# Gated linear attention before an MLP: each chunk of 128 tokens as two halves of 64 in different rows of the array

## The chip, the cores and the metric

One core of one Trainium2 chip runs the kernel. The metric is the device time in microseconds; before, the median of three runs is 577.57 us (577.46 to 578.66). All tensors are float32.

## The reference

Inputs q, k, v, alpha have the shape (batch 4, heads 8, tokens 768, head size 48). Per batch and head a 48x48 state runs over the tokens, and its reading feeds a two-layer MLP with weights 384x2048 and 2048x384:

```python
for t in range(S):
    state = alpha[:, :, t, :, None] * state + einsum('bhd,bhe->bhde', k[:, :, t], v[:, :, t])
    y[:, :, t] = einsum('bhd,bhde->bhe', q[:, :, t], state)
x = y.transpose(0, 2, 1, 3).reshape(3072, 384)
h = x @ w_in
out = (h * (1 / (1 + exp(-h)))) @ w_out
```

## The kernel before

The 768 tokens are cut into 6 chunks of 128 (`C`); with 4 batches that makes 24 (chunk, batch) units, called chunks here and numbered by `n`, with `ci` the chunk in its sequence and `b` the batch. Channels lie on partitions: two heads share a tile, one in rows 0 to 47 and one in rows 64 to 111 (`u` is 0 or 1), and four such pairs (`j`) lie side by side. The sequential gating is taken out of the attention with running products of alpha:

- `products(n)` brings alpha and k to a channels-by-tokens layout. Chunks 0 to 7 do it by TensorE transposes (L669); the later ones are loaded in a layout that VectorE's 32x32 transposes (L650) finish. A reversed scan (L674) makes `u`, for each token the product of the alphas after it, with the product of the whole chunk in a spare column (`c["all"]`). L681 multiplies k with it into `kp`.
- `quotient(n)` bounds the whole product from below (L696, `least`), takes its reciprocal (L697), scans forward from it (L699) and multiplies q with the result into `qp` (L704). Then kp and qp of one chunk need no more gating between them.
- `scores(n)` multiplies kp and qp per head (L715, 8 matmuls of 48 rows, 128x128), masks them to the causal half while copying from PSUM (L719, VectorE), transposes kp back to tokens-by-channels (L723), copies it (L725, `kn`) and scales the batch's state with the whole product (L729, four ScalarE multiplications).
- `values(n)` makes the output, transposed: 16 matmuls of 32 columns (v against the masked scores `g`) and, from the second chunk of a sequence on, 12 more (state against qp), all at L749, four column strips of the array at a time. L754 copies the result to `xt`, the MLP's input.
- `states(n)` multiplies kn and v (L764, 8 matmuls of 48x48) and adds the result to the state (L770, VectorE; L772, a ScalarE copy, in the first chunk).

A float32 matmul shows in the profile as two weight loads and two matmul passes, so the 8 matmuls of L715 in 24 chunks are x384.

The MLP's two matrix products run as "pieces" on the same TensorE: `enter_plain` (L807) and `enter` (L830, block products of sums of weight blocks and sums of inputs, with fewer multiplications than the plain form), and `leave` (L928) for the second product. VectorE makes the sums and differences that these need (L844, L919, L933, L546 and others), ScalarE evicts PSUM banks (L836) and applies the activation (L841). A loop over 25 steps with four slots each interleaves the two: each slot holds attention stages with their lag in chunks, `[(scores, 1)]`, `[(products, 0)]`, `[(values, 1), (states, 1)]`, `[(quotient, 0)]` from step 8 on, and after each slot `fill(step, slot)` issues as many pieces as are due by their planned work. In steps 0 to 3 products come before scores and states have slot 3; products of chunks below 8 include the quotient. A scheduler then orders each engine's instructions by their place in the program and their readiness, so an instruction can stand earlier in its queue than in the text; engines run their queues in order.

Buffers: attention's matmuls share a pool of three PSUM banks (`ps_attn`), used five times a chunk (two for scores, one for the transposes, one for values, one for states) and three times more for the transposes of chunks 4 to 7. The MLP has three banks of its own for the first product and two for the second. `u` and `p` (which hold kp and qp) have two buffers each. Loads, stores and the audit's loads (a check that alpha and the weights lie in the range that the scheme handles) are all issued from SP's queue, in order; v has two buffers, the late layout of alpha, k and q one each, refilled by `load(n + 1)` after `quotient(n)`.

Of the kernel before, what the change touches and what calls it, by code (L numbers as in the profile page):

```python
# [355 lines left out]
def quotients(  # L356
# [18 lines left out]

    nc = tc.nc
    pe, dve, act, gps = nc.tensor, nc.vector, nc.scalar, nc.gpsimd
    B, H, S, D = q.shape
    C = 128
# [7 lines left out]
    W = C + 1  # L387
# [20 lines left out]
    upool = pool("upool", 2)  # L408
    ppool = pool("ppool", 2)
# [39 lines left out]
    def load(n):  # L449
        c = ctxs.setdefault(n, dict(zip(("ci", "b"), divmod(n, B))))  # L450
        b, rows = c["b"], slice(c["ci"] * C, c["ci"] * C + C)
        for name, src in (("a", alpha), ("k", k), ("q", q)):
            x = src[b, :, rows, :]
            if n < NA:
                c[name] = nat[name][n % NIN]
                nc.sync.dma_start(c[name][:, :, 0:D], x.transpose([1, 0, 2]))
                continue

            c[name] = late["quads"][name]
            for u in range(2):
                for i in range(2):
                    r = 64 * u + 32 * i
                    nc.sync.dma_start(
                        c[name][r : r + 32, 32 * (1 - i) :][:, 0 : 4 * NP * D].rearrange(
                            "p (g c) -> p g c", g=NP),
                        x[u::2].rearrange("h (b j) d -> b h (j d)", j=4))
# [33 lines left out]

    seg = [(fix if i == 0 else spare).tile([128, NP * W + 1], F32, name=f"al{i}") for i in range(2)]
    inv = fix.tile([128, NP * W + 1], F32, name="inv")
    one = consts.tile([128, NP * W + 1], F32, name="one")
    gps.memset(seg[0], 0.0)
    gps.memset(one, 0.0)
    gps.memset(one[:, 0 : NP * W + 1 : W], 1.0)
    for t in [inv] + seg[1:]:
# [3 lines left out]
    mask = consts.tile([128, C], F32, name="mask")  # L513
    gps.memset(mask, 1.0)
    gps.affine_select(mask, mask, pattern=[[1, C]], compare_op=ALU.is_ge, fill=0.0, base=0,
                      channel_multiplier=-1)

    st = [fix.tile([128, NP, 2, D], F32, name=f"st{b}") for b in range(B)]
    for t in st:
        gps.memset(t, 0.0)  # L520
    least = fix.tile([128, NT, NP], F32, name="least")
# [122 lines left out]
    def tokens(t):  # L644

        return t[:, 1 : NP * W + 1].rearrange("p (j c) -> p j c", c=W)[:, :, 0:C]

    def turned(x, to):
        x = x[:, 32:].rearrange("p (g j d) -> p g j d", j=4, d=D)
        dve.transpose(to.rearrange("p g (b j) -> p g j b", j=4), x[:, :, :, 0:32])  # L650

    def products(n):
# [5 lines left out]
        for name in ("a", "k", "q"):  # L658
            if n >= NA:
                if name == "a":  # L660
                    turned(c[name], tokens(sg))
                continue
            if n < GB and name != "a":

                ps[name] = out_bank("kq".index(name), 512).rearrange("p (j c) -> p j c", c=C)
            else:
                ps[name] = ps_attn()
            for j in range(NP):
                pe.transpose(ps[name][:, j, :], c[name][:, 2 * j : 2 * j + 2, :], ident)  # L669
            if name == "a":  # L670
                act.copy(tokens(sg), ps[name])  # L671
        end = NP * W
# [4 lines left out]
        kp = c["kp"] = u[:, 1 : end + 1].rearrange("p (j c) -> p j c", c=W)[:, :, 0:C]  # L677
        if n >= NA:
            ps["k"] = late["turn"].tile([128, NP, C], F32, name="turn")
            turned(c["k"], ps["k"])  # L680
        dve.tensor_tensor(kp, ps["k"], kp, ALU.mult)  # L681
        c["all"] = u[:, 0:end:W]
# [5 lines left out]
    def quotient(n, sg=None, q=None):  # L688
# [6 lines left out]
        end, iv = NP * W, inv  # L695
        dve.tensor_single_scalar(least[:, n, :], c["all"], 2.0**-64, ALU.max)  # L696
        dve.reciprocal(iv[:, 0:end:W], least[:, n, :])  # L697
        p = ppool.tile([128, end + 1], F32, name="p")
        dve.tensor_tensor_scan(p[:, 0:end], sg[:, 0:end], iv[:, 0:end], 0.0, ALU.mult, ALU.add)  # L699
        qp = c["qp"] = tokens(p)  # L700
        if q is None:
            q = late["turn"].tile([128, NP, C], F32, name="turn")
            turned(c["q"], q)
        dve.tensor_tensor(qp, q, qp, ALU.mult)  # L704

    def scores(n):
        c = ctxs[n]
        ci, b = c["ci"], c["b"]
        ps = [ps_attn() for _ in range(2)]


        for j in range(NP):
            for u in range(2):
                r = slice(64 * u, 64 * u + D)
                pe.matmul(ps[u][:, j, :], lhsT=c["kp"][r, j, :], rhs=c["qp"][r, j, :],  # L715
                          start=True, stop=True)
        g = c["g"] = work.tile([128, 2, NP, C], F32, name="g")
        for u in range(2):
            dve.tensor_tensor(g[:, u], ps[u], mask[:, None, :].to_broadcast([128, NP, C]), ALU.mult)  # L719
        if ci < NCH - 1:  # L720
            ps_k = ps_attn()
            for j in range(NP):
                pe.transpose(ps_k[:, j, :], c["kp"][:, j, :], ident)  # L723
            c["kn"] = work.tile([128, NP, C], F32, name="kn")
            act.copy(c["kn"], ps_k)  # L725
        if ci > 0:
            s = st[b].rearrange("p j u e -> p j (u e)")
            for j in range(NP):
                act.mul(s[:, j], s[:, j], c["all"][:, j : j + 1])  # L729
# [4 lines left out]
    def values(n):  # L734
# [4 lines left out]
        s = st[b].rearrange("p j u e -> p j (u e)")  # L739
        py = ps_attn()  # L740
        todo = [(3 * j + i, vn[:, j, at : at + 32], g[:, u, j, :])
                for j in range(NP) for i, at, u in ((0, 0, 0), (1, 32, 0), (2, 80, 1))]
        todo += [(3 * j + 1, vn[:, j, 48:80], g[:, 1, j, :]) for j in range(NP)]
        if ci > 0:
            todo += [(3 * j + i, s[:, j, 32 * i : 32 * i + 32], qp[:, j, :])
                     for j in range(NP) for i in range(3)]
        for i, (at, w, x) in enumerate(todo):
            t, at = divmod(at, 4)
            pe.matmul(py[32 * at : 32 * at + 32, t, :], lhsT=w, rhs=x, start=(i < 4),  # L749
                      stop=(i >= len(todo) - 4), skip_group_check=True)  # L750
        half, e = divmod(n, 2)
        if e == 0:
            xts[half] = xtp.tile([128, NKT, TB], F32, name="xt")
        act.copy(xts[half][:, :, e * C : (e + 1) * C], py[:, 0:NKT])  # L754
    def states(n):
        c = ctxs.pop(n)
        ci, b, vn = c["ci"], c["b"], c["v"]
        if ci < NCH - 1:

            ps = ps_attn()  # L760
            for j in range(NP):
                for u in range(2):
                    r = slice(64 * u, 64 * u + D)
                    pe.matmul(ps[r, j, 0:D], lhsT=c["kn"][:, j, r], rhs=vn[:, 2 * j + u, 0:D],  # L764
                              start=True, stop=True)
            for u in range(2):
                r = slice(64 * u, 64 * u + D)
                s, x = st[b][r, :, u, :], ps[r, :, 0:D]
                if ci > 0:
                    dve.tensor_tensor(s, x, s, ALU.add)  # L770
                else:
                    act.copy(s, x)  # L772
# [329 lines left out]
    for step in range(STEPS):  # L1102
        stages = [[(scores, 1)], [(products, 0)], [(values, 1)], [(states, 1)]]
        if step < GB:

            stages = stages[1::-1] + stages[2:]
        elif step >= NA:
            stages = [[(scores, 1)], [(products, 0)], [(values, 1), (states, 1)], [(quotient, 0)]]
        for slot, group in enumerate(stages):
            for stage, lag in group:  # L1110
# [10 lines left out]
                if stage is states and n + NV < NT:  # L1121
# [25 lines left out]
    pe.matmul(ps, lhsT=good, rhs=mask[:, C - 1 : C], start=True, stop=True)  # L1147
# [63 lines left out]
```

## Time and profile before

| | |
|---|---|
| median of three runs | 577.57 us |
| the profiled execution | 578.95 us, span of the core 577.1 us |
| granted TensorE clock | 1.000 |
| VectorE transposes, L650 (48 in all) | 1.11 to 1.12 us each |
| scans, L674 and L699 (24 each) | 1.22 and 1.23 us each |
| load of alpha, late layout (64 issues) | 96 KB each, 2.3 us to landing |
| HBM read, written | 58.20 MB, 4.72 MB |

A line of a group reads: line of the code, engine, operation, output<-inputs, shape, count | busy time in us, mean ns of one | idle time of that engine just before, and what ended it. "PE" is a matmul on TensorE, "PEld" the load of its weights, DVE VectorE, ACT ScalarE. A mean of a matmul is its latency, not the distance to the next one, since passes overlap. A line of a timeline gives start, duration, what ran and how many. A line of stretches gives its bounds, its length, the busy time and count of PE, PEld, DVE, ACT and POOL, the granted clock, the DMA's share and its GB/s.

### The profile page before, as it was taken

How to read it: one execution, taken by the hardware profiler on the slowest of the kernel's cores; microseconds unless marked ns; L12 is line 12 of the kernel's file. 1: busy time of each engine (PE TensorE's matmuls, PEld its weight loads, DVE VectorE, ACT ScalarE, POOL GpSimd, SP SyncE). 2: the span in 40 equal slices, each digit the busy share in tenths (PEclk: the TensorE clock that was granted, in tenths of full speed). 3: DMA queues.
4: the chain of work that ended last, by engine and by line, in shares of the span. 5: the costliest groups of instructions: out<-in, count | busy, mean ns of one | idle time of the engine just before them, and what ended most of it. 6: DMA issues, size and time to landing. Idle time of an engine off the chain costs nothing. (4 is left out here: it accounts for less than half of the span.)

```text
span 577.1 us, 11060 instructions
## 1 busy us (share of the span) xinstructions
PE 557.6 (97%) x4450; PEld 491.2 (85%) x4450; DVE 449.3 (78%) x807; ACT 187.6 (33%) x367; POOL 7.3 (1%) x25
## 2 busy tenths in 40 slices
PE   5999999999999999999999999999999999998976
PEld 4677887678998998898998998998998999997976
DVE  5779798999797699995996995996963856747651
ACT  2345543232221233342442442433342331422100
POOL 5000000000000000000000000000000000000000
PEclk9999999999999999999999999999999999999999
DMA  9998784445445414343324333323210123333321
GB/s 212 169 285 215 212 215 118 102 103 139 103 99 129 116 51 120 107 124 84 103 71 118 101 105 85 101 69 89 65 43 9 52 81 115 93 118 98 98 72 30
DMA packets 93900, 63.72 MB, mean 110 GB/s; under 512 B 54800, under 2 KB 85520, under 8 KB 93840
## 3 DMA queue, kind: packets, MB, share of 16 engines
q1 hardware_dynamic: 93840, 62.94, 42.5%
q8 instruction: 36, 0.59, 0.4%
q14 instruction: 24, 0.20, 0.1%
HBM read 58.20 MB, written 4.72 MB: 109 GB/s over the span
## 5 line engine op out<-in xcount | busy, mean ns | idle before, releaser
L928 PE MATMUL ps_o<-w_out,g 128*128 128x192 f32 x704 | 122.8, 328 | 2.3 <-DVE o L942 2.2
L928 PEld LDWEIGHTS ps_o<-w_out,g 128*128 128x128 f32 x704 | 115.2, 190 | 5.6 <-DVE o L942 3.0
L928 PE MATMUL ps_o<-wt,g 128*128 128x192 f32 x528 | 91.6, 326 | 1.3 <-DVE u L1004 1.3
L807 PE MATMUL ps_m<-xt,w_in 128*128 128x256 f32 x384 | 89.6, 384 | 0.8 <-DVE w_in L604 0.5
L928 PEld LDWEIGHTS ps_o<-wt,g 128*128 128x128 f32 x528 | 87.2, 190 | 3.0 <-DVE u L1004 1.6
L807 PEld LDWEIGHTS ps_m<-xt,w_in 128*128 128x128 f32 x384 | 70.7, 190 | 12.2 <-DVE w_in L604 2.9
L830 PE MATMUL ps_m<-xc,w_in 128*128 128x256 f32 x288 | 70.1, 379 | 0.0
L639 DVE TENSOR_REDUCE seen<-bits 128x1 f32<-128x384 int32 (+2 forms) x65 | 42.4, 689 | 30.4 <-DMA bits<-in_moe_w_out_dram 23.9
L830 PEld LDWEIGHTS ps_m<-xc,w_in 128*128 128x128 f32 x288 | 54.0, 190 | 6.4 <-DVE g L844 0.2
L830 PE MATMUL ps_m<-xc,wx 128*128 128x256 f32 x192 | 50.1, 383 | 0.0
L836 ACT COPY g<-ps_m 128x512 f32<-128x512 f32 x64 | 37.0, 586 | 39.8 <-PE ps_m L830 39.8
L933 DVE TENSOR_TENSOR g<-g 128x512 f32<-128x512 f32 x66 | 44.7, 687 | 4.7 <-PE ps_o L928 4.7
L841 ACT ACTIVATE g<-g 128x1024 f32<-128x1024 f32 x32 | 33.2, 1056 | 44.6 <-DVE g L844 44.6
L729 ACT ACTIVATE st<-st,u 128x96 f32<-128x96 f32 x80 | 26.0, 368 | 53.5 <-DVE u L674 38.8
L844 DVE TENSOR_TENSOR g<-ps_m,g 128x512 f32<-128x512 f32 x56 | 37.6, 684 | 2.9 <-PE ps_m L830 2.7
L830 PEld LDWEIGHTS ps_m<-xc,wx 128*128 128x128 f32 x192 | 35.0, 190 | 4.2 <-issue 0.4
L719 DVE TENSOR_TENSOR g<-ps_a,mask 128x512 f32<-128x512 f32 x48 | 31.2, 685 | 6.4 <-PE ps_a L715 6.1
L674 DVE TENSOR_TENSOR_SCAN u<-al,one 128x516 f32<-128x516 f32 x24 | 29.3, 1224 | 6.2 <-ACT al L671 6.1
L699 DVE TENSOR_TENSOR_SCAN p<-al,inv 128x516 f32<-128x516 f32 x24 | 29.5, 1229 | 4.8 <-PE ps_a L749 4.2
L836 ACT COPY part<-ps_m 128x512 f32<-128x512 f32 x32 | 18.8, 587 | 43.6 <-PE ps_m L830 37.8
L810 ACT ACTIVATE g<-ps_m 128x512 f32<-128x512 f32 x32 | 19.0, 594 | 40.6 <-PE ps_m L807 40.5
L715 PEld LDWEIGHTS ps_a<-p,u 48*128 48x128 f32 x384 | 24.8, 193 | 8.1 <-issue 6.5
(117 smaller groups left out, 635.3 us busy)
## 6 DMA issues: line engine op xcount, KB each, us to landing
bits<-in_moe_w_in_dram SPq DMA_DIRECT2D x24, 512.0 KB, 4.2
bits<-in_moe_w_out_dram SPq DMA_DIRECT2D x32, 384.0 KB, 3.4
at<-in_alpha_dram SPq DMA_DIRECT2D x64, 96.0 KB, 2.3
kt<-in_k_dram SPq DMA_DIRECT2D x64, 96.0 KB, 2.4
qt<-in_q_dram SPq DMA_DIRECT2D x64, 96.0 KB, 2.5
vn<-in_v_dram SPq DMA_DIRECT2D x24, 192.0 KB, 3.5
bits<-in_alpha_dram SPq DMA_DIRECT2D x9, 512.0 KB, 3.9
out_dram<-o SPq DMA_DIRECT2D x48, 96.0 KB, 1.8
```

What stands on the lines that cost most here:

```text
L639: dve.tensor_reduce(seen[kind][which][:, i : i + 1], x, axis=AX, op=op, apply_absolute_value=True))
L674: dve.tensor_tensor_scan(u[:, end - 1 :: -1], sg[:, end:0:-1], one[:, end:0:-1], 0.0, ALU.mult, ALU.add)
L699: dve.tensor_tensor_scan(p[:, 0:end], sg[:, 0:end], iv[:, 0:end], 0.0, ALU.mult, ALU.add)
L719: dve.tensor_tensor(g[:, u], ps[u], mask[:, None, :].to_broadcast([128, NP, C]), ALU.mult)
L729: act.mul(s[:, j], s[:, j], c["all"][:, j : j + 1])
L807: pe.matmul(ps[:, e, :], lhsT=w_in[:, t, (f + e) * 128 : (f + e + 1) * 128], rhs=xt[:, t, :], start=(t == 0), stop=(t == NKT - 1))
L830: pe.matmul(ps[:, e], lhsT=block_w(w)[:, 2 * pair + e], rhs=block_x(grp, x), start=(first and e == 0), stop=(e == 1), skip_group_check=True)
L836: act.copy(to, ps)
L841: act.activation(x, x, AF.Silu)
L844: dve.tensor_tensor(to, a, b, op)
L928: pe.matmul(ps, lhsT=x, rhs=w[:, i], start=(first and i == 0), stop=(i == HF - 1), skip_group_check=True)
L933: dve.tensor_tensor(cells(grp, h, pair, *to), cells(grp, h, pair, *x), cells(grp, h, pair, *y), ALU.subtract)
```

## The change

A chunk stays 128 tokens, but the running products restart after 64 (`W = CH + 1`, eight segments `NS` instead of four). The scores of the two halves are 64x64 blocks: for both head parities and both halves, 16 matmuls go to the four quarters of the array. The mask is 64 wide. The weighted values run per half, its 64 tokens in its own rows of the array, and each half has its own output bank. A new tensor `mid` carries the state between the halves: the first half's states are added to the decayed old state into `mid`, `mid` is decayed with the second half's product, the second half of the values reads it, and the new state is `mid` plus the second half's states. So the states move ahead of the values, both halves' decays are ScalarE multiplications (`decay`), and the last chunk of a sequence makes transposes and first-half states too. Alpha's late load is split by halves (8 issues instead of 4). `u` has one buffer, and kp and qp live in tensors of their own, two each up to chunk 7 and one each afterwards (`turns`).

```diff
-    W = C + 1
+    CH = C // 2
+    W = CH + 1
+    NS = 2 * NP
...
-    upool = pool("upool", 2)
-    ppool = pool("ppool", 2)
+    upool = pool("upool")
...
+                    if name == "a":
+                        for e in range(2):
+                            nc.sync.dma_start(
+                                to.rearrange("p (g e c) -> p g e c", g=NP, e=2)[:, :, e],
+                                x[u::2, CH * e : CH * e + CH].rearrange("h (b j) d -> b h (j d)", j=2))
+                    else:
...
...
+    kps = [(spare if i else fix).tile([128, NP, C], F32, name=f"kp{i}") for i in range(2)]
+    qps = [(spare if i else fix).tile([128, NS * W + 1], F32, name=f"p{i}") for i in range(2)]
+    def turns(x, n):
+        return x[(n + 1) % 2 if n < NA else 0]
...
+    mid = [fix.tile([128, NP, 2, D], F32, name=f"mid{i}") for i in range(2)]
...
-        kp = c["kp"] = u[:, 1 : end + 1].rearrange("p (j c) -> p j c", c=W)[:, :, 0:C]
+        dve.tensor_single_scalar(least[:, n, :], u[:, 0:end:W], 2.0**-64, ALU.max)
+        kp = c["kp"] = turns(kps, n)
...
-        dve.tensor_tensor(kp, ps["k"], kp, ALU.mult)
+        dve.tensor_tensor(split(kp), split(ps["k"]), tokens(u), ALU.mult)
...
+    def decay(x, n, e):
+        x = x.rearrange("p j u e -> p j (u e)")
+        for j in range(NP):
+            act.mul(x[:, j], x[:, j], least[:, n, 2 * j + e : 2 * j + e + 1])
 
     def scores(n):
-        ps = [ps_attn() for _ in range(2)]
+        ps = [ps_attn(CH) for _ in range(2)]
+        for j in range(NP):
+            for u in range(2):
+                for e in range(2):
+                    r = slice(64 * u, 64 * u + D)
+                    pe.matmul(ps[u][CH * e : CH * e + CH, j, :], lhsT=c["kp"][r, j, CH * e : CH * e + CH],
+                              rhs=c["qp"][r, j, e, :], start=True, stop=True)
+        for u in range(2):
+            dve.tensor_tensor(g[:, u], ps[u][:, 0:NP], mask[:, None, :].to_broadcast([128, NP, CH]),
+                              ALU.mult)
...
+        if ci > 0:
+            decay(st[b], n, 0)
+
+    def states(n):
+        both = range(2) if ci < NCH - 1 else range(1)
+        ps = c["more"] = [ps_attn() for _ in both]
         for j in range(NP):
             for u in range(2):
+                for e in both:
+                    s = slice(CH * e, CH * e + CH)
+                    pe.matmul(ps[e][r, j, 0:D], lhsT=c["kn"][s, j, r], rhs=vn[s, 2 * j + u, 0:D],
+                              start=True, stop=True)
+        add(mid[n % 2], ps[0], st[b] if ci > 0 else None)
+        decay(mid[n % 2], n, 1)
+
+    def add(to, ps, old):
+        for u in range(2):
+            r = slice(64 * u, 64 * u + D)
+            s, x = to[r, :, u, :], ps[r, :, 0:D]
+            if old is None:
+                act.copy(s, x)
+            else:
+                dve.tensor_tensor(s, x, old[r, :, u, :], ALU.add)
 
     def values(n):
-        py = ps_attn()
+        py = [ps_attn(CH) for _ in range(2)]
+        todo = [(e, to, vn[CH * e : CH * e + CH, j, at : at + 32], g[CH * e : CH * e + CH, u, j, :])
+                for j, to, at, u in order for e in range(2)]
+        for e, x in ((0, st[b]), (1, mid[n % 2])):
+            if e == 1 or ci > 0:
+                todo += [(e, 3 * j + i, x[:, j, 32 * i : 32 * i + 32], qp[:, j, e, :])
+                         for j in range(NP) for i in range(3)]
...
+        for e in range(2):
+            act.copy(xts[half][:, :, odd * C + e * CH : odd * C + e * CH + CH], py[e][:, 0:NKT])
         if ci < NCH - 1:
+            add(st[b], c["more"][1], mid[n % 2])
...
-        stages = [[(scores, 1)], [(products, 0)], [(values, 1)], [(states, 1)]]
+        stages = [[(scores, 1)], [(states, 1), (products, 0)], [(values, 1)], [(quotient, 0)]]
         if step < GB:
-            stages = stages[1::-1] + stages[2:]
-        elif step >= NA:
-            stages = [[(scores, 1)], [(products, 0)], [(values, 1), (states, 1)], [(quotient, 0)]]
+            stages = [[(products, 0)], [(scores, 1), (states, 1)], [(values, 1)], []]
...
-                if stage is states and n + NV < NT:
+                if stage is values and n + NV < NT:
                     load_v(n + NV)
```

## The prediction

> **What bounds the kernel now.** I read the page's busy times first, then the groups of instructions with shapes apart, then the timeline of TensorE over one chunk, then busy times by stretch. The page:
>
> ```profile
> PE 557.6 (97%) x4450; PEld 491.2 (85%) x4450; DVE 449.3 (78%) x807; ACT 187.6 (33%) x367; POOL 7.3 (1%) x25
> ```
>
> TensorE is busy 97% of a span of 577.1 us at the full granted clock. Is it really full, or are its ends only modelled that way? The timeline of TensorE for one chunk (start, duration, instruction) answers:
>
> ```profile
> 305.60 0.98 PE L928 MATMUL ps_o<-wt,g 128*128 128x192 f32 x5
> 306.51 1.08 PE L749 MATMUL ps_a<-g,vn 128*32 128x128 f32 x32
> 307.41 0.84 PE L749 MATMUL ps_a<-p,st 128*32 128x128 f32 x24
> 308.18 0.56 PE L764 MATMUL ps_a<-vn,kn 128*48 128x48 f32 x16
> 308.67 1.13 PE L830 MATMUL ps_m<-xc,wx 128*128 128x256 f32 x4
> ...
> 316.65 1.16 PE L715 MATMUL ps_a<-p,u 48*128 48x128 f32 x16
> 317.74 0.66 PE L723 MATMUL ps_a<-ident,u 128*128 128x128 f32 x4
> 318.23 0.49 PE L928 MATMUL ps_o<-w_out,g 128*128 128x192 f32 x2
> ```
>
> Each float32 matmul is two recorded passes, and starts follow each other at about 0.83 ns per column plus 3 to 5: 216 ns for 256 columns, 163 for 192, 109 for 128, 45 for 48. Attention is four bursts between MoE work with no wait but the change of array layout. So time taken from a burst is time off the end, until another engine is late. Two stretches of 30 us (TensorE, weight loads, VectorE, ScalarE) show how near the next engine is:
>
> ```profile
> 210.00:240.00 30.00, 29.59 (x230) 26.74 (x229) 29.71 (x55) 9.11 (x20) 0.00 (x0) 1.00 0.43 119
> 300.00:330.00 30.00, 30.00 (x293) 27.15 (x291) 24.83 (x45) 11.72 (x23) 0.00 (x0) 1.00 0.45 121
> ```
>
> VectorE is full in the first and TensorE loses 0.41 us there; elsewhere it has 10 to 20% free. The groups that the change touches (busy, mean ns | idle before):
>
> ```profile
> L715 PE MATMUL ps_a<-p,u 48*128 48x128 f32 x384 | 30.0, 292 | 0.0
> L749 PE MATMUL ps_a<-g,vn 128*32 128x128 f32 x768 | 28.8, 282 | 1.0 <-ACT kn L725 0.7 <-DVE g L719 0.3
> L749 PE MATMUL ps_a<-p,st 128*32 128x128 f32 x480 | 17.0, 272 | 0.0
> L764 PE MATMUL ps_a<-vn,kn 128*48 128x48 f32 x320 | 11.9, 216 | 0.0
> L719 DVE TENSOR_TENSOR g<-ps_a,mask 128x512 f32<-128x512 f32 x48 | 31.2, 685 | 6.4 <-PE ps_a L715 6.1
> L770 DVE TENSOR_TENSOR st<-ps_a,st 48x192 f32<-48x192 f32 x32 | 11.1, 346 | 0.2
> L729 ACT ACTIVATE st<-st,u 128x96 f32<-128x96 f32 x80 | 26.0, 368 | 53.5 <-DVE u L674 38.8 <-DVE u L681 14.7
> ```
>
> **What the Trainium skill says.** "TensorE: Matmul & The Clock Gate", Part 3 (packing small matmuls): row and column tiles compose and run at once. The trace agrees for one direction at a time: two rows in the scores (starts 7 ns apart, pairs every 109 ns), four columns in the values (fours every 109 ns); both at once no run here shows. The same page, "Wait — 56ns, not 53.3ns?", puts a floor of about 25 ns between starts however small the matmul; in the trace different tiles start 7 ns apart, so it cannot hold across tiles. "TensorEngine Tiling (Array Packing)", Key Properties: a change of tiling mode drains the array. The trace agrees: 91 to 107 ns at each. Its "Gotcha 1: PSUM Pressure" wants different row tiles in different banks; the change does that (a bank per head parity in the scores, per half elsewhere).
>
> **The change, part by part (TensorE).** A 64-column pass isn't in the trace; between 48 columns (45) and 128 (109) it is 58 ns. Per chunk:
> - Scores: 8 pairs x 109 become 8 fours x 58: -0.41 us.
> - Weighted values (g): 8 fours x 109 become 8 eights x 58: -0.41.
> - State part of the values: 6 fours x 109 become 12 x 58, since each half reads its own state: +0.04. In the 4 first chunks, which had none, 6 x 58: +0.35.
> - States: 8 pairs x 45 become 8 fours x 45: 0. The 4 last chunks had none and now make the middle state: +0.36, and 4 transposes x 109: +0.44.
> - Layout changes. Before, each as gap plus the first, longer step: MoE to scores 91+105, scores to transposes 100+56, MoE to values 92+25, values to states 91+35, states to MoE 96+103: 0.79. After, states are a burst of their own and g and state parts need different row layouts: 144 (half the columns to load), 156, 131 and 199 for states, 119+118+199 for values: 1.07. So +0.27; in the last chunks, which had 0.72, +0.35.
>
> Sums: 16 middle chunks x -0.51 = -8.1; 4 first x -0.20 = -0.8; 4 last x +0.37 = +1.5. Together -7.4 us. Bounds of the unknown pitch: 53 ns (64 columns at 0.83) gives 28 steps x 4.6 x 24 chunks = 3.1 us more; above, 69 ns takes all of it (28 x 11 x 24 = 7.4). I take the interpolation, since both its ends are bursts of this kind.
>
> **VectorE.** Masks: 48 of 256 elements, by the 128x256 rows (420) for 685: -12.7 us. Additions of states: 80 instead of 32, at 346: +16.6. The scans grow from 516 to 520 elements, the minimum and reciprocal from 4 to 8: nothing to speak of. Net +4 us in 449, hidden where VectorE has room; in the full stretches (some 3 chunks' time) 0.2 us a chunk comes through, 0.5 in all. Without any cover it is 4.
>
> **ScalarE.** 96 more decays at 368 (35 us), 24 x (2 x 314 - 472) for the split copy of the output, 4 x 585 for the added copies of kn: +41 us, to 40%. Hidden as work. As a wait it isn't: states, two additions (0.7), four decays (starts 270 apart, 1.2) must end before the last 24 passes of the values; with hops some 2.4 us against the MoE work of a slot, at least one piece of 2.5 us, mostly two. Behind the decays wait the evictions of the MoE banks (three of them) and behind these TensorE. I allow 1 us over the kernel.
>
> **DMA and SP.** Alpha comes in eight loads instead of four for 16 chunks, each row piece halved to 384 bytes: 64 issues x 0.43 = 27 us of SP's queue, 1.7 us a chunk, ahead of k, q, the stores and the audit's loads. In the trace alpha's buffer is refilled at 312.7 and read at 333.5: 20 us of slack, so zero; with that gone it would be 1.7 a chunk. The load of v moves from behind the states to behind the values, which stood together: zero.
>
> **Buffers.** u is single, and from chunk 8 on kp and p too. kp's readers (transposes at 317.7) already come before the next product (321.6), p's readers (values at 306.5) before the next scan (308.3): no new order, zero; the bound is one scan, 1.2 us, on VectorE, with its evictions behind. Score banks: 7 takes a chunk for 5, from three, and one is held from the states to the end of the values. In steps 4 to 7, where the products take three more, the values now wait for the products' end: copy 0.59, scan 1.22, product 0.69, scan 1.23, product 0.69, small ones 0.34: 4.8 us for the 3.1 that lie between now (70.98 to 74.10). MoE work of later slots can be put there; I take 0.2 a step, 1 us in all with the waits of the later steps; without cover 1.7 x 4 = 7.
>
> **Start.** The first MoE matmul (26.87) waits for chunk 1's output. New behind its transposes (22.5): copy of kn 0.6, states 0.4, two copies 0.64, four decays 1.2, state part 0.4, copy 0.3, which ends near 27.3 for 26.7 now: +0.5.
>
> Sum: -7.4 +0.5 +1 +1 +0.5 = -4.4. The profiled execution took 578.95 (577.1 of span, 1.85 around it), so it would take 574.6; the median of the runs lies 1.4 under it: 577.57 - 4.4 = 573.2.
>
> **Rivals.** (1) The queue of TensorE cannot sustain one pair of load and matmul every 7 ns: the trace shows that rate for bursts of eight weight loads (306.51 to 306.56), and for longer only 22.5 ns (states). g needs 7.2, states 11, the rest 14. At r ns a pair, g costs 8 x (8r - 58) more, and so on; near 10 the gain is gone (4.3 us), at 15 it is 0.66 us a chunk, 16 us: 589. For it: nothing faster is shown over 16 pairs. Against: no pass in the bursts shows it. (2) Waits: the 7 us of steps 4 to 7 uncovered, and as little as 1 us more from decays: some 580; it decides once stalls beyond those allowed pass 4.4 us. For it: three banks, VectorE at 90% in these steps; against: TensorE never waits above 1 us between 30 and 500 us. (3) The halves don't run at once where rows and columns are split (the change not doing what it says): g costs 16 x 58, 0.46 lost on the forecast, 11 us: 584. (4) All covered but the start, and the pitch 53: 577.57 - 10.5 + 0.5 = 567.6, some 568. For it: the 128-column fours come within 2.3 ns of their columns' time; against: the 48-column pairs don't, by 5.
>
> **Numbers.** Forecast 0.44 (its own range 571 to 576.5), (1) 0.18, (2) 0.24, (3) 0.06, (4) 0.08. The range 568 to 588 leaves out half of (1) and some of (4). A measurement tells 0.2% (1.15 us) from no change. Faster: most of the forecast and (4), 0.50; within 0.2%: edges of the forecast and of (2), 0.11; slower 0.39.
>
> **What would show it.** The scores' burst 0.4 us shorter before its transposes, fours 58 ns apart; g in eights at 58; five layout changes around the states and values costing 0.77. Right also: no idle time of TensorE on banks ps_a or on decays. Wrong if g's passes follow at 10 ns or more, if steps 4 to 7 are longer than the 15.7 us of now, or if evictions wait behind decays.

## The result and the profile after

The changed kernel takes 603.45 us, median of four runs (601.65 to 604.75), against 577.52 us of the kernel before beside it: a ratio of 1.0442, 95% interval 1.0412 to 1.0473. The forecast was 573.2 us, range 568 to 588. (What the forecast calls MoE work is the MLP's.) The profiled execution has a span of 599.9 us, 22.8 more than before.

The page's busy times of the changed kernel:

```profile
PE 565.6 (94%) x6578; PEld 491.9 (82%) x6578; DVE 452.7 (75%) x855; ACT 219.5 (37%) x491; POOL 8.3 (1%) x28
```

These times count overlapping instructions once. The forecast added up durations, and by that measure ScalarE's work grew by 40.9 us (199.0 to 239.9), for a forecast of 41, while VectorE's fell by 1.1 us (497.1 to 496.0), for a forecast of +4. The masks and the additions came out as forecast; the difference is a gain that the forecast didn't see: VectorE's transposes of alpha, whose load is now split by halves, take 0.71 us instead of 1.12, 6.6 us over 16 chunks. TensorE's idle time has grown from 19.5 to 34.3 us, but that is not all: the ends of its passes are modelled, so I add up the distances from the start of each pass to the next one. Before they come to 567.6 us, now to 590.3. The columns of all passes, at 0.83 ns each and divided by the number that run at once, come to some 515 and 498 us. So the halves did save some 17 us of columns, and some 40 us of something else came in.

The timeline of TensorE around one chunk of the changed kernel (start, duration, instruction) shows the bursts:

```profile
287.53 0.58 PE L771 MATMUL ps_a<-vn,kn 64*48 64x48 f32 x32
288.03 2.87 PE L975 MATMUL ps_o<-wt,g 128*128 128x192 f32 x16
290.83 0.86 PE L810 MATMUL ps_a<-g,vn 64*32 64x64 f32 x64
291.62 0.54 PE L810 MATMUL ps_a<-p,st 128*32 128x64 f32 x24
291.98 0.52 PE L810 MATMUL ps_a<-p,mid 128*32 128x64 f32 x24
292.43 1.89 PE L975 MATMUL ps_o<-w_out,g 128*128 128x192 f32 x10
```

Where nothing is late, the bursts are as forecast, but for g: its 64 passes take 0.79 us up to the state part. Eights every 58 ns would take 0.46 and a change of layout.

Where things are late is seen in the waits. TensorE's and GpSimd's of the changed kernel (what waited <- for what: us in all, times, longest):

```profile
PE ps_a L745 <- DVE p L727: 9.8, 5, 6.2
PE ps_a L810 <- DVE mid L783: 4.3, 7, 1.0
PE ps_a L810 <- DVE p L727: 2.3, 2, 1.2
POOL at L1129 <- DVE st L783: 102.5, 1, 102.5
```

TensorE waits 6.2 us in one piece for a chunk's qp, from 203.6 to 209.8 us. Before, no wait of TensorE between 30 and 500 us passed 1 us. And GpSimd clears alpha's late buffer, `at`, only at 109.4 us; before, it did so at 5.7. What follows from that, on SP's queue and VectorE:

```profile
110.21 4.68 SPq L472 DMA_DIRECT2D at<-in_alpha_dram  x8
114.99 1.80 SPq L476 DMA_DIRECT2D kt<-in_k_dram  x4
116.89 1.80 SPq L476 DMA_DIRECT2D qt<-in_q_dram  x4
118.73 3.75 SPq L472 DMA_DIRECT2D at<-in_alpha_dram  x8
122.53 3.32 SPq L476 DMA_DIRECT2D kt<-in_k_dram  x4
125.89 1.85 SPq L476 DMA_DIRECT2D qt<-in_q_dram  x4
```

```profile
134.53 0.69 DVE L966 TENSOR_TENSOR g<-g 128x512 f32<-128x512 f32 x1 [8.63 <-ACT g L857]
135.14 0.70 DVE L671 STREAM_TRANSPOSE al<-at 128x512 f32<-128x512 f32 x1
```

Chunk 8's alpha, k and q are loaded at 110 us and then all over again. Its gating begins at 135.1 us (before: 92.3) and its scores at 150.4 (before: 127.6). The stretches of 30 us (TensorE, weight loads, VectorE, ScalarE, GpSimd, granted clock) show what that costs. Two of the kernel before, then four of the changed one:

```profile
90.00:120.00 30.00, 30.00 (x261) 19.64 (x260) 27.71 (x46) 7.73 (x20) 0.00 (x0) 1.00 0.38 85
120.00:150.00 30.00, 30.00 (x286) 25.40 (x286) 24.74 (x41) 10.08 (x24) 0.00 (x0) 1.00 0.52 127
```

```profile
90.00:120.00 30.00, 28.78 (x435) 18.25 (x434) 16.28 (x33) 8.88 (x26) 2.17 (x3) 1.00 0.29 72
120.00:150.00 30.00, 30.00 (x246) 25.77 (x244) 13.03 (x22) 7.81 (x19) 0.00 (x0) 1.00 0.25 63
180.00:210.00 30.00, 23.27 (x287) 20.50 (x289) 23.69 (x46) 9.03 (x23) 0.00 (x0) 0.94 0.39 98
210.00:240.00 30.00, 26.66 (x436) 23.41 (x436) 27.11 (x60) 9.78 (x25) 0.00 (x0) 0.95 0.36 94
```

From 90 to 150 us VectorE works 29.3 of 60 us; before it was 52.5. TensorE is still full until 150, with MLP pieces; after that it waits for what VectorE didn't do then, and from 180 to 240 us loses 10 of 60 us.

The second loads have a plain reason in the diff. The new list of stages has `(quotient, 0)` from step 4 on. For chunks 4 to 7 `quotient` returns at once, since products did its work, but the loop then calls `load(n + 1)` again. The list of DMA issues counts `an`, `kn` and `qn` eleven times instead of eight, and 61.15 MB are read from HBM for 58.20.

### The profile page after: what moved, and what is told of

It is laid out like the page before. It is cut to its first block, busy times and chain, and to the rows that moved or that the text cites. A ratio compares the mean times of both kernels' runs of the same rounds, so it can differ in the third digit from the quotient of the medians.

```text
span 599.9 us, 15625 instructions
## 1 busy us (share of the span) xinstructions
PE 565.6 (94%) x6578; PEld 491.9 (82%) x6578; DVE 452.7 (75%) x855; ACT 219.5 (37%) x491; POOL 8.3 (1%) x28
## 3 DMA queue, kind: packets, MB, share of 16 engines
HBM read 61.15 MB, written 4.72 MB: 110 GB/s over the span
## 5 line engine op out<-in xcount | busy, mean ns | idle before, releaser
L975 PE MATMUL ps_o<-w_out,g 128*128 128x192 f32 x704 | 124.3, 330 | 1.9 <-DVE o L989 1.2
L975 PE MATMUL ps_o<-wt,g 128*128 128x192 f32 x528 | 94.2, 328 | 1.1 <-DVE u L1051 0.8
L854 PE MATMUL ps_m<-xt,w_in 128*128 128x256 f32 x384 | 88.1, 382 | 0.1
L980 DVE TENSOR_TENSOR g<-g 128x512 f32<-128x512 f32 x66 | 43.5, 687 | 4.1 <-PE ps_o L975 4.1
L733 ACT ACTIVATE mid<-mid,least 128x96 f32<-128x96 f32 x96 | 28.1, 363 | 29.2 <-DVE mid L783 29.1
L698 DVE TENSOR_TENSOR_SCAN u<-al,one 128x520 f32<-128x520 f32 x24 | 29.7, 1237 | 6.7 <-ACT al L695 6.3
L810 PE MATMUL ps_a<-g,vn 64*32 64x64 f32 x1536 | 27.2, 225 | 7.1 <-DVE mid L783 4.3
L810 PEld LDWEIGHTS ps_a<-g,vn 64*32 64x32 f32 x1536 | 21.0, 107 | 13.7 <-issue 8.3
L733 ACT ACTIVATE st<-st,least 128x96 f32<-128x96 f32 x80 | 23.4, 363 | 20.4 <-DVE least L701 20.3
L722 DVE TENSOR_TENSOR_SCAN p<-al,inv 128x520 f32<-128x520 f32 x24 | 29.8, 1240 | 1.4
```

The lines of the kernel that those rows point to most:

```text
L698: dve.tensor_tensor_scan(u[:, end - 1 :: -1], sg[:, end:0:-1], one[:, end:0:-1], 0.0, ALU.mult, ALU.add)
L733: act.mul(x[:, j], x[:, j], least[:, n, 2 * j + e : 2 * j + e + 1])
L810: pe.matmul(py[e][32 * at : 32 * at + 32, t, :], lhsT=w, rhs=x, start=(i < starts), stop=(last[e, at] == i), skip_group_check=True)
L854: pe.matmul(ps[:, e, :], lhsT=w_in[:, t, (f + e) * 128 : (f + e + 1) * 128], rhs=xt[:, t, :], start=(t == 0), stop=(t == NKT - 1))
L975: pe.matmul(ps, lhsT=x, rhs=w[:, i], start=(first and i == 0), stop=(i == HF - 1), skip_group_check=True)
L980: dve.tensor_tensor(cells(grp, h, pair, *to), cells(grp, h, pair, *x), cells(grp, h, pair, *y), ALU.subtract)
```

## The experiments

**1. Second loads or shared memory.** The idea of the second cause: `kp1` and `p1` are new in the memory that is given up after chunk 7, and the late buffers, which are opened over that memory, now lie in part on them, so that `at` cannot be cleared before chunk 6 has been read. (No run prints the addresses; what shows it is the run with separate pools under 2.) Three runs were to take the two causes apart. Beside this and all later runs the kernel before took 578.45 to 578.74 us, and ratios are against that. No second loads (e1_no_reload):

```diff
-                if stage is quotient and n + 1 < NT:
+                if stage is quotient and NA <= n < NT - 1:
```

> The changed kernel without the loads that it issues twice: as changed, steps 4 to 7 have the slot (quotient, 0), after which load(n + 1) runs a second time, also for chunk 8, whose alpha, k and q are so loaded twice. Theory A (the second loads make chunk 8 late, and what follows is the queueing up of the late chunks): 580 to 586 us, chunk 8's scores start before 135 us instead of 150. Theory B (the late layout of alpha now lies on the memory of kp1 and p1, so that its memset and its load wait for chunk 6): still 595 or more, the memset of GpSimd still after 100 us. Theory C (short passes cannot be issued fast enough, and the added waits do the rest, evenly over the kernel): 600 or more.

Measured: 588.55 us, ratio 1.0182 (1.0153 to 1.0211). The second loads (theory A) are worth 15 us, and 10 us above the kernel before are left. GpSimd's clearing still comes at 109.1 us. The other order of the three late buffers, q first (e1_quads_clear):

```diff
-        late["quads"] = {name: quads.tile([128, 32 + 4 * NP * D], F32, name=f"{name}t") for name in "akq"}
-        for name, t in late["quads"].items():
-            gps.memset(t, 1.0 if name == "a" else 0.0)
+        late["quads"] = {name: quads.tile([128, 32 + 4 * NP * D], F32, name=f"{name}t") for name in "qak"}
+        for name in "akq":
+            gps.memset(late["quads"][name], 1.0 if name == "a" else 0.0)
```

> The changed kernel with the three tensors of the late layout allocated in another order, so that only q's (the last one needed) shares memory with kp1 and p1; every engine's instructions keep their order. Theory A (second loads): 595 to 603 us, since the second load of chunk 8's alpha is still waited for. Theory B (shared memory): 580 to 588, chunk 8's scores before 135 us. Theory C (issue rate and waits everywhere): 600 or more.

Measured: 604.04 us, 1.0420 (1.0391 to 1.0448). No verdict on B: alpha's clearing stays at 108.7 us. The three buffers are tiles of one pool, and it looks as if what lies under any of them is waited for before the first is written (the next runs bear this out); the edit did not part what it was to part. So the run with both edits, e1_both, tells no more than the first:

> Both edits together: no second loads and no shared memory under alpha's late layout. If A or B or the two together are the cause, 577 to 582 us: the kernel before (577.5), less 7.4 for the shorter bursts, plus 7 for g (0.79 us a chunk against the 0.49 forecast, 24 times), plus some 3 for added waits; chunk 8's scores near 128 us. Theory C: over 592 us, with the waits of TensorE spread evenly.

Measured: 590.12 us, 1.0195 (1.0154 to 1.0235), cleared at 111.8 us.

**2. Pools of their own.** Now each late buffer has a pool, q's first, so that alpha's and k's share nothing (e2_apart, without the second loads too):

```diff
-        quads = pool("quads")
-        late["quads"] = {name: quads.tile([128, 32 + 4 * NP * D], F32, name=f"{name}t") for name in "akq"}
+        late["quads"] = {name: pool(f"{name}pool").tile([128, 32 + 4 * NP * D], F32, name=f"{name}t")
+                         for name in "qak"}
...
```

> The changed kernel without the second loads, and with the late layout's three tensors in pools of their own, q's first: only q's memory now reaches into that of kp1 and p1. In the run without second loads GpSimd's memset of alpha's tensor still waited for chunk 6 (109 us), and in the run with the other order of the three too (111.8), since the one pool that held all three was waited for as a whole. Theory B2 (the memory that the late layout shares makes chunk 8's gating late, 118 us for 92 before, and VectorE, which idles 5.5 us at 109, has to make up for it until 390): memset before 10 us, chunk 8's alpha transposed before 100 us, TensorE's waits between 170 and 390 us (8 us in the run without second loads) gone, 577 to 582 us. Theory D (single buffers of u, kp and p, and more work on VectorE): 585 to 590, the same waits at the same places.

Measured: 580.22 us, 1.0031 (1.0020 to 1.0042). Alpha's and k's buffers are cleared early again, and only q's still waits, as it must if it alone lies on `kp1` and `p1`. Chunk 8's alpha is transposed at 92.3 us, as before. The instructions on alpha's late buffer, and GpSimd's clearing of q's:

```profile
L671 DVE STREAM_TRANSPOSE al<-at x16: 701/704/711, 92.3 to 419.4; 128x512 f32<-128x512 f32 x16
L1128 POOL MEMSET at<- x1: 757/757/757, 6.8 to 6.8; 128x800 f32 x1
```

```profile
110.65 0.76 POOL L1128 MEMSET qt<- 128x800 f32 x1 [102.36 <-ACT xt L816]
```

The same edit with the second loads left in (e3_reload_apart):

> The changed kernel with the second loads kept and only the late layout's tensors in pools of their own, q's first. Without the second loads this edit was worth 8.3 us (588.5 to 580.2). If chunk 8's second load of alpha, which follows chunk 7's quotient, is what holds its gating in any case, the memory is worth nothing here: 600 to 604. If the two delays add up: 593 to 596.

Measured: 589.53 us, 1.0199 (1.0180 to 1.0218), better than either forecast of mine. So shared memory alone costs 8.3 us (588.55 against 580.22), second loads alone 9.3 (589.53 against 580.22), both 23.2 (23.8 by the ratios, since the kernel before was 1.2 us faster beside the changed kernel). They stand in one chain, clearing, first loads, second loads, gating, and either alone ends at about the same place: q of chunk 8, the last to be loaded, is transposed at 128.1 and 126.2 us, both together at 148.4, neither at 118.0. Whether alpha alone is late matters less: two runs below (e2_apart_prod, e5_out_last) transpose it at 113.4 and 110.6 us, but q at 117.2 and 114.3, and are not slower than the runs that they start from.

**3. The same faults in the kernel before.** Each was put into chunks of 128 tokens, where no halves are:

> The kernel before with one edit: steps 4 to 7 get the empty stage (quotient, 0), after which load(n + 1) runs a second time, as in the changed kernel. No work is added but the loads (for chunk 8 alpha, k and q twice, for 5 to 7 once more in the early layout). Theory A: 585 to 595 us, chunk 8's scores 10 us or more later than 127.6. If the second loads are harmful only together with the changed kernel's buffers: 577 to 580.

> The kernel before, chunks of 128 tokens, with the changed kernel's buffers alone: one u, kp and p in tensors of their own, two each up to chunk 7 and one afterwards, so that the late layout of alpha lies on the memory of kp1 and p1. Forecast of the prediction (no new order, zero): 577 to 579. Theories B2 and D: 582 to 588, with chunk 8's alpha transposed after 105 us for 92.

Measured: 582.60 us, 1.0068 (1.0051 to 1.0085), with second loads (e2_before_reload); 577.10 us, 0.9982 (0.9966 to 0.9998), with the changed kernel's buffers (e2_before_bufs). Here the second loads cost 3.9 us, less than theory A had said, and chunk 8's scores are not late (127.3 us). The trace, of the fastest of the four executions (580.45 us), shows one long wait in the middle and what it brings:

```profile
226.51 1.03 PE L830 MATMUL ps_m<-xc,wx 128*128 128x256 f32 x4
229.86 1.40 PE L830 MATMUL ps_m<-xt,wx 128*128 128x256 f32 x4 [2.33 <-DVE g L844]
231.05 1.91 PE L830 MATMUL ps_m<-xc,w_in 128*128 128x256 f32 x4
```

Four passes that start 216 ns apart elsewhere take 1.2 and then 1.8 us: in the stretches of 1 us the granted clock is 0.80 from 230 us, 0.50 up to 234 and 1.00 again from there. So the wait of 2.3 us costs some 1.7 us more, 4.0 in all. This execution as a whole is only 1.7 us above the kernel before, so the wait doesn't account for the 3.9 of the medians; no other of the four was traced.

The buffers cost nothing there, as the prediction's zero has it, although chunk 8's alpha is transposed at 118.1 and its q at 128.3 us, as late as in the run without second loads. So lateness alone doesn't do it; in the kernel with the halves it costs 8.3 us. That fits with what the halves put on VectorE between one burst and the next (80 additions of states for 32), but which part of it turns the delay into time no run here shows.

**4. Waits for banks in steps 4 to 7.** In these steps the transposes for alpha, k and q take three more of the attention's banks. Products behind the values (e2_apart_prod):

```diff
+        elif step < NA:
+            stages = [[(scores, 1)], [(states, 1)], [(values, 1), (products, 0)], []]
```

> As the one before, and in steps 4 to 7 the products are issued behind the values, not ahead of them, so that no values wait for a bank of the products (1.37 and 1.29 us at 73 and 90 us in the run without second loads, and 0.88 at 58). If these waits cost what they show: 2 to 3.5 us less than the run before it. If the products come too late for the scores of the next step in their turn, or chunk 8's gating does: no gain, or slower.

Measured: 579.08 us, 1.0005 (0.9997 to 1.0012), 1.1 less than e2_apart, between its two forecasts. Of the waits inside the values one of 0.8 us is left; transposes that wait for the values' banks, four times 0.8 us, took their place. One stage a slot (e3_apart_mid):

```diff
+        elif step < NA:
+            stages = [[(scores, 1)], [(products, 0)], [(states, 1)], [(values, 1)]]
```

> As e2_apart (no second loads, late layout in pools of their own), and steps 4 to 7 in the order scores, products, states, values, one stage a slot with MLP work between all of them, so that neither states nor values wait for a bank of the products (in e2_apart TensorE lost 1.37, 1.28, 1.27 and 1.69 us to waits inside the values at 74 to 140 us, in e2_apart_prod 0.8 us seven times). If these waits are what keeps the halves from their gain: 574 to 577 us, faster than before by 0.3 to 0.8%. If the halves' short passes are worth nothing in themselves: 578 to 580, like e2_apart_prod.

Measured: 583.26 us, 1.0094 (1.0073 to 1.0114): a miss. The scheduler mixed the bursts, and TensorE waits in the middle of them for states that VectorE hasn't added yet:

```profile
107.23 0.65 PE L810 MATMUL ps_a<-g,vn 64*32 64x64 f32 x32
107.81 0.30 PE L810 MATMUL ps_a<-p,st 128*32 128x64 f32 x2
110.11 1.04 PE L810 MATMUL ps_a<-g,vn 64*32 64x64 f32 x32 [1.99 <-DVE mid L783]
111.08 0.76 PE L810 MATMUL ps_a<-p,st 128*32 128x64 f32 x19
```

Behind this wait of 2.0 us, and behind another at 534 us, the granted clock stands at 0.50 for 3.41 us each, which is 3.4 us of work lost in all.

Then banks that nobody needs. The MLP's second product leaves its two banks idle until 93 us, so k's and q's transposes of chunks 4 to 6 can go there, as those of chunks 0 to 3 do (e4_apart_out, e4_prod_out and, on the kernel before, e4_before_out):

```diff
-            if n < GB and name != "a":
+            if n < GB + 3 and name != "a":
```

> As e2_apart, and the transposes of k and q of chunks 4 to 6 go to the two banks of the MLP's second product, which stand idle until 93 us, as those of chunks 0 to 3 do. So the values of these steps wait for no bank of the products (0.89, 1.37, 1.28 us at 58, 73 and 90 us in e2_apart). If the bursts' gain (5 us by the burst lengths) is eaten by waits in steps 4 to 7: 577 us, 3 less than e2_apart's 580.2. If VectorE takes what TensorE is freed of, as in e3_half_g: no change, 580.

> As e2_apart_prod, and k's and q's transposes of chunks 4 and 5 in the idle banks. It takes away two waits of 0.8 us and shortens two. Waits are the cause: 577 to 578 (579.1 without). VectorE is: 579.

> The kernel before with k's and q's transposes of chunks 4 to 6 in the idle banks, and nothing else: the control for e4_apart_out. The kernel before shows no wait for a bank between 40 and 230 us, so both theories expect no change: 577.5 to 579.5.

Measured: on e2_apart 577.55 us, 0.9984 (0.9975 to 0.9993); on e2_apart_prod (chunks 4 and 5 only) 578.73, 1.0005 (0.9996 to 1.0014); on the kernel before 577.78, 0.9984 (0.9974 to 0.9994). The first is 2.7 us less than without the edit, as the theory of bank waits has it. But the kernel before gains 0.9 us (by the ratio) from the same edit, though its trace shows no wait for a bank there, so that not all of the 2.7 need be waits of the halves; and the second, 0.35 us less, can't be told from no change, where that theory had 1 to 2 us. So these runs alone don't prove it. The halves, repaired so far, come out even with the control. What was left in e4_apart_out, TensorE's groups for g and its timeline in step 9, with VectorE beside it:

```profile
L810 PE MATMUL ps_a<-g,vn 64*32 64x64 f32 x1536 | 22.8, 226 | 2.9 <-DVE mid L783 1.5 <-DVE p L727 1.1
```

```profile
136.59 0.30 PE L810 MATMUL ps_a<-g,vn 64*32 64x64 f32 x2
137.53 0.72 DVE L783 TENSOR_TENSOR mid<-ps_a,st 48x192 f32<-48x192 f32 x2
138.40 0.83 PE L810 MATMUL ps_a<-g,vn 64*32 64x64 f32 x62 [1.51 <-DVE mid L783]
```

The states ended at 133.5, but their addition stands behind 4 us of other work in VectorE's queue, about half of it sums of weights for the MLP. Until then the states hold the bank that the second half's values need, and the burst stops after two passes. The other wait, 1.27 us at 104 us, is for a bank of chunk 7's products. For step 7 alone, products behind the values (e5_out_last):

```diff
+        elif step == NA - 1:
+            stages = [[(scores, 1)], [(states, 1)], [(values, 1), (products, 0)], []]
```

> As e4_apart_out, and in step 7 alone the products are issued behind the values, since there the idle banks are taken. It takes away the wait of 1.27 us at 104 us inside chunk 6's values. If bank waits are what keeps the gain of the bursts back: 576.3, 1.2 less than e4_apart_out's 577.55. If chunk 8's gating, which comes later for it (113 us or so for 91.5), matters as it did in e1_no_reload: 578 to 580.

Measured: 576.07 us, 0.9957 (0.9943 to 0.9970), 1.5 less, though chunk 8's alpha is transposed at 110.6 us again. It beats the kernel before by 0.4%, and the control (0.9984) by 0.27%, some 1.6 us; the two intervals just miss each other (0.9970 and 0.9974). Its line for g shows the waits gone; passes and their work are the same:

```profile
L810 PE MATMUL ps_a<-g,vn 64*32 64x64 f32 x1536 | 22.3, 227 | 0.5 <-ACT mid L781 0.2 <-DVE g L749 0.2
```

**5. How fast pairs of a load and a pass are issued.** TensorE alone (e1_bursts):

> No attention and no MLP: the output is zeros. TensorE alone runs nine bursts of short matmuls, each behind eight dense ones of 128x128x256. Columns are the rows and columns of the array that one takes and its N; 64 matmuls are 128 pairs of a load and a pass. If a pair can be issued every 7 ns for as long as one likes (the forecast), 64x32 N=64 takes 16 x 58 ns = 0.93 us. If the fast pairs come from a queue that empties (seen in g after the change: 32 pairs at 7 ns, then 13 to 18 ns), it takes 0.25 + 96 x 14 = 1.6 us or more, and with N=128 (fours of 14 ns a pair) it is no slower than its columns, 16 x 109 = 1.75 us. 128x32 N=64, half as many at once, needs 14 ns a pair, and comes out at 32 x 58 = 1.86 us under both unless the steady rate is slower than 14; 128x32 N=32 would need 7.7 and then takes as long as N=64.

Measured, TensorE's timeline (columns as before):

```profile
10.43 1.48 PE L53 MATMUL ps<-x,w 64*32 64x64 f32 x128
15.49 1.99 PE L53 MATMUL ps<-x,w 128*32 128x64 f32 x128
26.74 2.03 PE L53 MATMUL ps<-x,w 64*32 64x128 f32 x128
37.53 1.30 PE L53 MATMUL ps<-x,w 128*32 128x32 f32 x128
42.40 0.86 PE L53 MATMUL ps<-x,w 64*32 64x64 f32 x64
54.28 14.40 PE L53 MATMUL ps<-x,w 128*128 128x64 f32 x128
```

The burst of 64 takes 0.86 us here as in the kernel, so g's length is its own and owes nothing to waits. Start to start, its first 32 passes take 0.27 us; then come one gap of 56 ns and 30 passes in 0.32 us, 12 ns a pass with the gap; in the burst of 128 the third quarter takes 0.30 us, 9.4 ns a pass. With N=128 (14 ns needed) the columns set the pace: 0.44 us per 32. With 128x32 and N=32, where 7.7 are needed, 32 pairs take 0.27 to 0.29 us: it is not as slow as with N=64 (0.45), which I had expected, and it doesn't slow down after 32. So beyond the first 32 a pair takes 9.4 to 12 ns on tiles of 64x32, and 8.3 to 9.1 throughout on tiles of 128x32, not 13 to 18; one rate for all tiles is not what the bursts show.

Does that time count in the kernel? Half of g's matmuls left out (e3_half_g):

```diff
+        if ci > 0:
+            del todo[len(todo) // 2 :]
```

> As e2_apart_prod, but from the fifth chunk on, half of the matmuls of the weighted values are left out (16 of 32, 32 passes of 64), so the outputs lack two of the four head pairs' share. Forecast of the prediction (eights every 58 ns): 20 chunks x 4 x 58 ns = 4.6 us less than the 579.1 of e2_apart_prod: 574.5. Issue theory (the first 32 pairs at 7 to 8 ns, the others at 12, as in the bursts alone: 0.27 and 0.38 us): what is left out is the slow half, 20 x 0.38 = 7.6 us less: 571.5. In the trace the burst ends after 0.42 us with the change of layout instead of 0.79.

Measured: 582.86 us, 1.0081 (1.0062 to 1.0100), slower than 579.08 with all of them. The burst itself does what the issue theory says:

```profile
175.84 0.45 PE L812 MATMUL ps_a<-g,vn 64*32 64x64 f32 x32
176.22 0.55 PE L812 MATMUL ps_a<-p,st 128*32 128x64 f32 x24
```

0.38 us to the next burst instead of 0.79: the second 32 passes cost 0.40 a chunk, where the forecast had 0.23. The distances within the attention's passes fall from 107.2 to 100.0 us, and those of the MLP rise from 460.3 to 471.0. The largest of TensorE's waits in that run:

```profile
PE ps_o L977 <- DVE o L991: 7.0, 7, 2.4
```

So 7 us less of TensorE brought nothing: its waits, most of them for VectorE, grew by 7.5 us between 30 and 500 us, and behind the longest, of 2.4 us, stands a stretch of 3.41 us at half clock, which costs 1.7 us more. The scheduler also gave all engines another order, and so this run doesn't tell how much of the 10.7 us is VectorE's limit and how much a bad order.

## Why the prediction was wrong

**DMA and SP: the step that failed first.** The forecast read the new stage list for the order of the halves, and wrote "zero" against the loads, from 20 us of slack in the middle of the kernel. It did not ask what else hangs on a stage that has become empty. In steps 4 to 7 `load(n + 1)` runs twice, for which the forecast has zero and the runs show 15 us of the changed kernel's time (e1_no_reload), 9.3 where the memory is apart (e3_reload_apart) and 3.9 in the kernel before (e2_before_reload). The slack was that of a late chunk, too; chunk 8, the first in the late layout, has a chain of its own.

**Buffers: "no new order, zero".** The order of readers and writers was looked at, the memory not. The late buffers came to lie on `kp1` and `p1`: 8.3 us more. In the kernel before the same buffers cost nothing (577.10), so it takes the halves to make this dear; how they do it stays open. With both steps mended the ratio falls from 1.0442 to 1.0031: they are over nine tenths of what the change costs.

**Steps 4 to 7: right in place, too small.** 1 us was allowed for banks in all, with 7 as the bound. In e2_apart the values wait three times for 1.3 us (74, 91 and 108 us), the scores once for 0.9, and step 9's values 1.7. The idle banks and step 7's order took 4.2 us off the time (580.22 to 576.07); 0.9 of that the idle banks give the kernel before as well.

**TensorE's sum: right in sign, some 15% off per middle chunk, with one term wrong.** From start to start in undisturbed chunks, each with the change of layout behind it:

| per chunk, us | before | halves | forecast of the difference |
|---|---|---|---|
| scores | 1.093 | 0.626 | -0.41 and its layout |
| g | 0.897 | 0.787 | -0.41 and its layout |
| state part | 0.771 | 0.810 | +0.04 and its layout |
| states, and one more change from MLP work | 0.495 | 0.597 | 0 and +0.09 |
| scores to states, with transposes and entries | 3.93 | 3.50 | -0.51 |

So -0.44 for -0.51. The term that was mis-sized is g: 12 ns a pass in its second half for the 7.25 of "8 eights x 58", 0.17 us a chunk. The other terms together came out 0.1 us better than forecast, so that the sum is closer than its parts by luck. Over the kernel the distances from start to start, without the waits above 0.3 us between 30 and 500 us, fall by 6.9 us from the kernel before to e4_apart_out (567.6 - 1.7 = 565.9 to 565.7 - 6.7 = 559.0) against the 7.4 forecast. The start cost 0.2 us for 0.5: the first MLP pass comes at 27.04 us instead of 26.87.

**ScalarE and VectorE.** ScalarE's work was right (+40.9 us for 41), and no eviction behind the decays shows among the longer waits. VectorE's work was put 5 us too high, for want of the shorter transposes of alpha; its wait was put too low, at 0.5 us in all. In the wait of 1.5 us shown above the additions do not hurt by their work but by where they stand in the queue: a bank stays held until they have run.

**The rivals.** (1) holds in kind, not in size: g's pairs do slow down after 32, to 12 ns, which prices g at 24 x 0.17 = 4 us, not 16. (2) is what happened, by a cause that it did not name and far beyond its 580. (3) is refuted: in g's burst the middle eights follow each other at 55 to 57 ns, with rows and columns split, and g takes 0.79 us where it would need 0.93. (4) did not come. Of the signs that I had asked for, those of the bursts were seen (the scores' burst shorter, fours at 58 ns; and for wrong, g's passes at over 10 ns). "No idle time of TensorE on banks ps_a" failed, by the 6.6 us that values wait for `mid` and `p` of others to free a bank (L810 above). None of the signs covers the longest wait, the 6.2 us for qp at 203 us; that no wait above 1 us appears would have been the better test.

With both faults and most bank waits mended, the ratio of 0.9957 makes 575.1 us of the 577.57 that the forecast started from: 573.2 was forecast, with its own range of 571 to 576.5. Against the control with the same idle banks the repaired halves gain some 1.6 us, where the forecast had 4.4; the shorter bursts are there, and the waits take most of them back.

## What to carry to other kernels

When a loop's list of stages changes, go through everything that hangs on each stage, loads above all, also for steps in which the stage itself does nothing. When buffers move, look up what later lies on their memory: a pool that is opened over freed space waits for all of it, and this shows as one early instruction with a very long wait (102 us of GpSimd). When TensorE is full and the next engine has 10% left, count each new wait for that engine's queue, not only its added work.

## What the runs showed of the hardware

- **Pairs of load and pass.** On tiles of 64x32 with N=64 (e1_bursts, and g in the kernel) the first 32 pairs start 6 to 9 ns apart within their eights and take 0.27 us; after that a pair takes 9.4 to 12 ns. On tiles of 128x32 with N=32 it is 8.3 to 9.1 ns from the first pair on. 32 pairs are 64 instructions. The Trainium skill, "TensorE: Matmul & The Clock Gate", section "Architectural detail: the array is 16× 32×32, not 1× 128×128", gives TensorE's queue 64 entries; the number agrees, but no run here changed the queue or showed that it is the cause, and the tiles of 128x32 don't slow down at 32, though their spacing turns uneven there too.
- **The clock drops by windows, not by waits.** In these traces the granted clock changes on a grid of 3.413 us: the stretches of 0.50 inside the runs last 3.41, 6.83 or 13.65 us, and the two of e3_apart_mid begin at 110.20 and 536.87 us, 125 such windows apart. Lay this grid over every trace in which the clock changes, from 8.5 us on (the first passes run at half pace, with no record of the clock), and add up TensorE's idle time in each window, up to the ends of passes as the profile models them. All 12 windows at full clock with 1.99 us of idle time or more were followed by half clock; none of the 2614 with 1.92 us or less was. So it matters where a wait falls:

| waits of TensorE | idle time in one window | clock behind it |
|---|---|---|
| 2.33 us up to 229.86 (e2_before_reload) | 2.33 | 0.50, 230.59 to 234.00 |
| 1.99 us up to 110.11 (e3_apart_mid) | 1.99 | 0.50, 110.20 to 113.62 |
| two of 1.01 us, up to 382.98 and 385.09 (e3_reload_apart) | 2.02 | 0.50, 385.29 to 388.70 |
| 2.17 us up to 530.90 (before) | 1.92, the rest in the window ahead | 1.00 |
| 2.51 us up to 220.05 (e1_both) | 1.81, the rest in the next window | 1.00 |

A window at half clock, if TensorE is busy in it, costs 1.7 us of work. "TensorE: Matmul & The Clock Gate" of the Trainium skill, section "What's actually happening", states half the clock after an idle window of some 3.4 us, and windows that run freely. The length and the free running agree; but here a window need not be idle throughout, 1.99 us of it were enough.

- **Full-size weights with few columns.** Passes of 128x128 with N=64 start 112 ns apart (the burst of 14.40 us), and the transposes of 128x128 with N=128 in the kernel before 109 ns apart, so that half the columns save nothing. On tiles of 128x64 with N=64 they start 29 ns apart, a pair every 58. That the load of the full-size weights sets this pace is likely; no run here shows it.
